# The last 16 rows of Y and Z: made once for all batches, two batches to a group of 32 partitions

## The chip, the core and the metric

The kernel runs on one core of a Trainium2 chip. A core has a matrix engine (TensorE, PE in the profile, its weight loads PEld), a vector engine (VectorE, DVE), a scalar engine (ScalarE, ACT), a general engine (GpSimd, POOL) and an engine for synchronization (SyncE, SP). Transfers are issued by SP, ACT or POOL and carried by 16 DMA engines. The metric is the device time of one execution in microseconds (us). Before the change it is 435.41 us, the median of three runs (435.04, 435.41 and 435.62 us).

## The reference, cut to what matters

```python
# attention: q, k, v are (8 batches, 8 heads, 576 positions, 64), float32
scores = q @ k^T / 8, kept where 0 <= row - column < 64
x = softmax(scores) @ v, laid out as (8, 576, 512)
# spectral mix: w_r, w_i are (64 modes, 512, 512); w_ch is (512, 512)
X = rfft(x, axis=1)[:, :64]
Yr = Xr @ w_r - Xi @ w_i        # per mode
Yi = Xr @ w_i + Xi @ w_r
y = irfft(Yr + 1j * Yi, n=576, axis=1)
u = x + y
out = u + max(u @ w_ch, 0)      # (8, 576, 512), float32
```

The weights are 134 MB, the attention's inputs 28 MB, and the output is 9.44 MB. As u @ w_ch = x @ w_ch + irfft(Y) @ w_ch, the kernel forms Z = Y @ w_ch on the 128 spectral rows (64 modes, real and imaginary part) and adds its inverse transform to x @ w_ch.

## The kernel before, in words

Attention comes first, unit by unit, with the weights of the modes streaming in beside it. The weights are cast to bf16 on the way by transfers that POOL issues, 1 MB at the receiving side each, into two rings of buffers (ringA, ringB) and into lent tiles; L152 to L165 issue the next one when a buffer has been spent. Each group of four modes is multiplied at L188 (`mode_half`), and `finish_group` (L630) turns its 8 spectral rows (4 modes, two parts) for all 8 batches into place. Rows of the spectrum are partitions: `Yall` and `Zall` hold 128 rows by 8 batches by 512 columns, Y in bf16 and Z in 32 bit.

Groups 12 and 13 (`LAST` and `LAST + 1`) are multiplied last. They own rows 96 to 111 of the spectrum, called `rows`, the last 16 rows of the title. Everything else of Y and Z is complete before the last weights land: `batch_job` (L682) makes `Yall` and `Zall` of a batch with these 16 rows at zero, `early_jobs` (L730) already add the inverse transform of those 112 rows to the tiles of batches 0 to 3, in `UE` (for u) and `XW` (for x @ w_ch). The 36 tiles of the output have 128 rows by 512 columns. 16 of them, four for each of batches 0 to 3, are the early tiles; the other 20 are full tiles.

After the last weights the code from L994 runs. For the early tiles the 16 late rows are held apart: batch by batch on their own partitions, YL (bf16, groups of 32 partitions of which 16 are used, batches 0 to 3 at 64, 96, 0, 32, see `YG`) and ZL (at 0, 32, 64, 96, see `ZG`). `trigL` and `trigLr` hold the matching 16 rows of the inverse transform's table once in each of the four groups; eight transfers that SP issues at L951 and L952 put them there, in the middle of the weight stream. `pick` is a 0/1 matrix that moves the rows of the four batches to their groups, `sel` one that compacts the rows of all batches. For the full tiles the late rows have to be in `Yall` and `Zall`: a second product by `sel` (`put_y`, L651) gives them for all batches, ACT casts it into `yst` (L1010), one SP transfer of 128 KB brings them into `Yall` (L1011); a second product with w_ch (L1015, from `trl`) gives the rows of Z, ACT casts them into `zst` (L1020), and one SP transfer of 256 KB brings them into `Zall` (L1021).

`seq` is the order of the tile pairs: four early pairs, then full and early pairs in turn, then full pairs. An early pair (`early`, L903) needs two products with K = 16 for u (L796) and two for z (L803), an addition on DVE (L829), a relu on ACT (L834) and an addition on POOL (L835). A full pair (`full_u`, `full_z`) adds the table's product with `Yall` (L849, L854) and with `Zall` (L868). `plan` puts the output transfers in an order by estimated times. Most are issued by SP at L821, some of the full tiles by ACT. SP takes its instructions in the order of the program, so an issue that waits for its tile holds all that come later.

Of the kernel before, what the change touches and what calls it, by code (L numbers as in the profile page):

```python
# [9 lines left out]
FP32 = mybir.dt.float32  # L10
# [16 lines left out]
def kernel(  # L27
# [10 lines left out]
    nc = tc.nc  # L38
# [32 lines left out]
    pick = consts.tile([128, 32 * NLB + 8], BF16, name="pick")  # L71
# [125 lines left out]
    with tc.manual_schedule():  # L197
# [223 lines left out]
        def trig_steps():  # L421
            yield lambda: ve.memset(trigF[64:128, NTC - 1, :], 0.0)
            yield lambda: ve.memset(trigF[0:64, NTC, :], 0.0)

            yield lambda: ve.tensor_copy(out=sel, in_=ident.rearrange("p (g x) -> p g x", x=32)[:, :, 0:16])
            yield lambda: ve.memset(pick, 0.0)
            yield lambda: zero_xq(1, ve)
            for to in range(0, NLB, 2):
                b = (to + 2) % NLB
                yield lambda to=to, b=b: ve.tensor_copy(  # L430
                    out=pick[:, 8:].rearrange("p (b x) -> p b x", b=NLB)[:, to:to + 2, 0:8].rearrange("p b (g r) -> p b g r", g=4),
                    in_=sel.rearrange("p g (r b) -> p b g r", b=B)[:, b:b + 2])

        trig = list(trig_steps())
        pp = pool("pp", bufs=2, reuse_waits="tile")
# [90 lines left out]
        trigL = zpool.tile([128, 4 * 128], BF16, name="trigL")  # L526
        trigLr = zpool.tile([128, 4 * 128], FP32R, name="trigLr")
        trl = zpool.tile([128, NDCH, 128], FP32R, name="trl")
        trz = zpool.tile([128, NDCH, NLB, 32], FP32R, name="trz")
# [3 lines left out]
        rowpool = pool("rowpool", reuse_waits="tile")  # L533
# [55 lines left out]
        YT = Yall.rearrange("p b (c k) -> p b c k", c=NDCH)  # L589

        rows = slice(8 * LAST, 8 * LAST + 16)
        YG, ZG = (64, 96, 0, 32), (0, 32, 64, 96)

        def yrows(b):
            return Yall[:, b, :]
# [34 lines left out]
        def finish_group(grp, psm):  # L630
            stg = stgpool.tile([128, DM], BF16, name="stg")
            if grp == LAST + 1:
                cast_halves(stg, psm)
            elif grp < EARLY:
                nc.vector.tensor_tensor(out=stg, in0=psm, in1=Yacc[grp], op=ALU.add)  # L635
            else:
                nc.vector.tensor_copy(out=stg, in_=psm)
            i = grp % 2
            end = grp - i == LAST
            if i == 0:  # L640
                late["pt"] = bank("p", [128, NDCH, 128])
                late["py"] = bank("y") if end else None
            pt, py = late["pt"], late["py"]
            lanes = sel.rearrange("p g x -> p (g x)")
# [6 lines left out]
            def put_y():  # L651
                nc.tensor.matmul(out=py[64 * i:64 * i + 64, :], lhsT=lanes, rhs=stg, start=True, stop=True,
                                 tile_position=(0, 64 * i))

            def put_first():
                nc.tensor.matmul(out=late["first"], lhsT=pick[:, 8 - 8 * i:136 - 8 * i], rhs=stg,
                                 start=(i == 0), stop=(i == 1))

            def take():
                nc.scalar.copy(out=trl[:, :, 64 * i:64 * i + 64], in_=pt[:, :, 64 * i:64 * i + 64])  # L660

            def take_first():
                nc.scalar.copy(out=trz[:, :, :, 8 * i:8 * i + 8],
                               in_=pt[:, :, 64 * i:64 * i + 64].rearrange("p c (r b) -> p c b r", b=B)[:, :, 0:NLB])

            def prepare():
                turn()
                if end:
                    put_y()
                    take_first()  # L670
                    take()
                elif i:
                    k0 = 8 * (grp - 1)
                    nc.scalar.copy(out=YT[:, :, :, k0:k0 + 16], in_=pt.rearrange("p c (k b) -> p b c k", b=B))

            if end:
                late[i] = turn, put_first, take, put_y, take_first
            if not (end and i):
                ready.append(prepare)

# [79 lines left out]
                 [XQ[hb].rearrange("p s b m -> p (s b m)").bitcast(FP32).rearrange("p (t e) -> p t e", e=DM)]  # L760
                 for i in range(4)]
        UE_OF = {tile_of(b, c) for b in range(NLB) for c in range(4)}
        AA = [(18 * k // 2 + c, 18 * k // 2 + 4 + c) for k in range(NLB // 2) for c in range(4)]
        BB = [(8, 17), (26, 35)] + [(i, i + 1) for k in range(NLB // 2, B // 2) for i in range(9 * k, 9 * k + 8, 2)]
        assert sorted(i for p in AA + BB for i in p) == list(range(NT))
        X4 = [BB.pop(0) for _ in range(2)]
# [25 lines left out]
        def late_u(n):  # L792
            for i in seq[n]:
                (at, b), = tiles[i][1]
                r = slice(YG[b], YG[b] + 16)
                nc.tensor.matmul(out=pu[i], lhsT=trigL[r, at:at + 128], rhs=YL[r], start=True, stop=True,  # L796
                                 tile_position=(YG[b], 0))

        def late_z(n):
            for i in seq[n]:  # L800
                (at, b), = tiles[i][1]
                r = slice(ZG[b], ZG[b] + 16)
                nc.tensor.matmul(out=ps[i], lhsT=trigLr[r, at:at + 128], rhs=ZL[r], start=False, stop=True,  # L803
                                 skip_group_check=True, tile_position=(ZG[b], 0))

        by_act = {(i, 1) for p in X4 for i in p} | {(p[1], 0) for p in BB[:-1]}
        behind = []
# [128 lines left out]
        for i, (grp, hb) in enumerate(steps[EARLY:]):  # L936
            f, l = grp < EARLY or hb == 0, hb == 1
            if i == EARLY:
                while tables:
                    tables.pop(0)()  # L940
                while jobs or pend:
                    advance()
                close(stmp2, yp, ringB)
                Zall = pool("zall", side="right").tile([2 * NM, B, DM], FP32R, name="Zall")
                x_jobs(pool("xp1", side="right", reuse_waits="tile"), NX0, NT)
                utpool = pool("utpool", side="right", reuse_waits="tile")
                nc.vector.memset(YT[:, :, :, rows], 0.0)
                nc.vector.tensor_scalar(out=trz.rearrange("p c g k -> p c (g k)"), scalar1=0.0, scalar2=None, op0=ALU.mult,
                                        in0=ident.unsqueeze(1).to_broadcast([128, NDCH, 128]))
                for g in range(4):  # L950
                    nc.sync.dma_start(out=trigL[32 * g:32 * g + 16], in_=trigI[rows, 0:512])  # L951
                    nc.sync.dma_start(out=trigLr.bitcast(FP32)[32 * g:32 * g + 16], in_=trigIr.bitcast(FP32)[rows, 0:512])  # L952
                given = 0
            if f:
                psm = [bank("m"), bank("m")] if grp == LAST + 1 else bank("m")
# [35 lines left out]

        turn, put_first, take, put_y, take_first = late[1]  # L994
        tr, first = trl, late["first"]
        turn()
        take_first()
        put_first()
        put_y()
# [11 lines left out]
        nc.sync.dma_start(out=Yall[rows], in_=yst)  # L1011
# [9 lines left out]
        nc.sync.dma_start(out=Zall.bitcast(FP32)[rows], in_=zst.bitcast(FP32))  # L1021
# [43 lines left out]
```

## Time and profile before

| | us |
|---|---|
| median of three runs | 435.41 |
| the profiled execution's own time | 435.39 |
| its span, first to last instruction | 433.6 |
| last weights consumed by PE from | 396.66 |
| first output issued by SP at | 403.17 |
| last product of PE | about 427 |

| engine | busy us | share of the span |
|---|---|---|
| PE | 327.2 | 75% |
| DVE | 229.8 | 53% |
| ACT | 180.1 | 42% |
| POOL | 101.2 | 23% |

The queue q0 carries what POOL issues (the weights and the inputs of the attention, 81.73 MB at the receiving side), q1 what SP issues, q10 what ACT issues. In a timeline a row gives the start and the length in us, the engine, the line, the operation with out<-in, and how many instructions were merged. A q behind an engine's name means its sequencer, which issues transfers. In a row of windows come the busy time of each engine with the number of instructions, the granted TensorE clock, the busy share of the 16 DMA engines (it can go over 1, since packets of one engine overlap) and GB/s.

### The profile page before, as it was taken

To read this page: it belongs to the slowest core of one execution; us is meant where nothing else is said; L and a number is where in the kernel's file an instruction comes from. 1 tells how busy PE (TensorE), PEld (TensorE's weight loads), DVE (VectorE), ACT (ScalarE), POOL (GpSimd) and SP (SyncE) were. 2 spreads that over 40 slices of the span, in tenths; PEclk is the share of its full clock that TensorE was granted. 3 is DMA by queue.
4 is the path that set the end of the run, shared out by engine and by line. 5 is a ranking of instruction groups with operands and counts; after the bars stand their busy time and mean duration, and the time that the engine had idled before them with its cause. 6 is when DMAs were issued, how large, how long until landed. Compare 5 with 4: busy or idle time off the path is not lost.

```text
span 433.6 us, 11034 instructions
## 1 busy us (share of the span) xinstructions
PE 327.2 (75%) x4802; PEld 214.6 (49%) x4802; DVE 229.8 (53%) x472; ACT 180.1 (42%) x322; POOL 101.2 (23%) x150
## 2 busy tenths in 40 slices
PE   6999999998999999963208343767584668779993
PEld 3666667576667666641104121444353345445652
DVE  8588787876776776863104111122131325752994
ACT  5665757565666666520201100122121213434842
POOL 8322222222131231122102100012111112110990
PEclk8899999999999999996557768588889989999998
DMA  8999999999999999999999999999999999993798
GB/s 203 212 211 212 211 211 213 210 211 212 212 213 211 212 212 211 212 213 211 212 259 212 218 212 212 212 210 212 212 209 212 211 212 212 212 212 77 245 365 288
DMA packets 47280, 93.64 MB, mean 216 GB/s; under 512 B 2688, under 2 KB 3136, under 8 KB 47232
## 3 DMA queue, kind: packets, MB, share of 16 engines
q0 software_dynamic: 41008, 81.73, 99.7%
q1 hardware_dynamic: 5328, 9.77, 6.6%
q10 hardware_dynamic: 896, 1.44, 0.9%
q8 instruction: 37, 0.61, 0.5%
q14 instruction: 11, 0.09, 0.1%
HBM read 163.58 MB, written 9.44 MB: 399 GB/s over the span
## 4 chain that ended last, share of the span: by engine, by line
DMA 51%; PE 36%; issue 5%; ACT 3%; DVE 3%; POOL 1%; DVEq 0%; POOLq 0%
DMA wi<-in_moe_w_i_dram 29%; DMA wr<-in_moe_w_r_dram 22%; PE tr L231 6%; PE s L278 4%; PE s L270 3%; PE s L290 3%; PE pt L298 3%; PE psm L188 3%; PE vb L243 3%; PE o L318 2%; PE psz L786 1%; PE pst L786 1%; PE pst L868 1%; PE psz L610 1%; PE px L341 1%
## 5 line engine op out<-in xcount | busy, mean ns | idle before, releaser
L610 PE MATMUL psz<-wch,tr 128*128 128x512 f32 x176 | 62.3, 486 | 11.7 <-DMA wch<-in_moe_w_ch_dram 11.0
L756 DVE CAST xw<-psz 128x512 fp32r<-128x512 f32 x36 | 24.9, 692 | 86.1 <-PE psz L610 86.1
L584 ACT CAST tr<-ptx 128x512 fp32r<-128x512 bf16 x36 | 21.1, 586 | 104.1 <-PE ptx L603 104.1
L282 DVE TENSOR_REDUCE mx<-s 128x4 fp32r<-128x512 f32 x72 | 49.6, 688 | 27.0 <-PE s L278 26.7
L188 PEld LDWEIGHTS <-XQ 128*32 128x32 bf16 x448 | 18.8, 175 | 79.2 <-issue 55.9
L188 PE MATMUL psm<-wi,XQ 128*32 128x512 bf16 x208 | 20.1, 461 | 37.6 <-DMA wi<-in_moe_w_i_dram 37.6
L165 POOL DMA_DIRECT2D wi<-in_moe_w_i_dram x32 | 23.4, 732 | 102.8 <-PE psm L188 74.7
L610 PEld LDWEIGHTS psz<-wch,tr 128*128 128x128 f32 x176 | 36.8, 232 | 18.8 <-issue 11.5
L292 ACT ACTIVATE p<-s 128x512 bf16<-128x512 f32 x72 | 39.7, 603 | 12.9 <-PE s L290 12.9
L165 POOL DMA_DIRECT2D wr<-in_moe_w_r_dram x27 | 20.2, 749 | 97.0 <-PE psm L188 49.0
L188 PE MATMUL psm<-wr,XQ 128*32 128x512 bf16 x184 | 17.9, 465 | 28.3 <-DMA wr<-in_moe_w_r_dram 27.4
L235 ACT COPY kT<-tr 128x576 bf16<-128x576 bf16 x32 | 23.2, 724 | 21.1 <-PE tr L231 21.1
L278 PE MATMUL s<-kT,qT 64*64 64x128 bf16 (+1 forms) x576 | 29.2, 221 | 0.0
L270 PE MATMUL s<-mask_t,ident_bf 128*128 128x512 bf16 x72 | 28.4, 395 | 0.9 <-ACT p L292 0.8
L301 DVE COPY pts<-pt 128x1024 bf16<-128x1024 bf16 (+1 forms) x40 | 25.2, 629 | 5.0 <-PE pt L298 3.6
L235 ACT COPY qT<-tr 128x576 bf16<-128x576 bf16 x32 | 23.3, 728 | 10.6 <-PE tr L231 10.6
L278 PEld LDWEIGHTS <-qT 64*64 64x64 bf16 x576 | 17.8, 107 | 18.0 <-issue 17.5
L635 DVE TENSOR_TENSOR stg<-psm,Yfour 128x512 bf16<-128x512 f32 x10 | 6.9, 690 | 36.8 <-PE psm L188 36.8
L290 PE MATMUL s<-mx,ident_r 128*128 128x512 f32 x72 | 26.2, 437 | 0.0
L235 ACT COPY vT<-tr 128x576 bf16<-128x576 bf16 x32 | 23.3, 727 | 4.3 <-PE tr L231 4.2
L298 PE MATMUL pt<-ident_bf,p 128*128 128x128 bf16 x288 | 23.3, 220 | 1.7 <-issue 1.6
L218 POOL DMA_DIRECT2D rawk<-in_k_dram x15 | 8.1, 539 | 65.3 <-PE tr L231 59.1
(217 smaller groups left out, 607.4 us busy)
## 6 DMA issues: line engine op xcount, KB each, us to landing
wi<-in_moe_w_i_dram POOLq DMA_DIRECT2D x29, 1024.0 KB, 18.6
wr<-in_moe_w_r_dram POOLq DMA_DIRECT2D x27, 1024.0 KB, 17.9
out_dram<-ut SPq DMA_DIRECT2D x23, 256.0 KB, 2.8
rawv<-in_v_dram POOLq DMA_DIRECT2D x16, 288.0 KB, 15.0
rawk<-in_k_dram POOLq DMA_DIRECT2D x15, 288.0 KB, 14.1
rawq<-in_q_dram POOLq DMA_DIRECT2D x15, 288.0 KB, 14.0
x_sb<-in_moe_w_r_dram POOLq DMA_DIRECT2D x2, 1024.0 KB, 15.9
out_dram<-utx SPq DMA_DIRECT2D x5, 256.0 KB, 3.1
```

Source lines behind the costliest of these rows:

```text
L165: nc.gpsimd.dma_start(out=w[:, to:to + len(ps)], in_=src[ps[0]:ps[-1] + 1, HALF * hb:HALF * hb + HALF, :].rearrange("g (p j) e -> p g j e" ...
L188: nc.tensor.matmul(out=ps[32 * g:32 * g + 32, 0:e], lhsT=of.rearrange("k s b m -> k (s b) m")[:, (3 * j + 1 - ri) * B:(3 * j + 5 - ri) * B ...
L231: nc.tensor.transpose(out=pt[ro, j, :], in_=raw[ro, TH * half + j, :], identity=ident_bf[ro, ro])
L235: nc.scalar.copy(out=to, in_=pt.rearrange("p j n -> p n j"))
L270: nc.tensor.matmul(out=s, lhsT=ident_bf, rhs=mask_t[:, mk], start=True, stop=True)
L278: nc.tensor.matmul(out=s[ro, t, lo:128], lhsT=lq, rhs=kT[ro, 64 * n - 64 + lo:64 * n + 64], start=False, stop=True, skip_group_check=True)
L282: nc.vector.tensor_reduce(out=mx, in_=s, axis=AX.X, op=ALU.max, negate=True)
L290: nc.tensor.matmul(out=s, lhsT=ident_r, rhs=mx.unsqueeze(2).to_broadcast([128, 4, 128]), start=False, stop=True, skip_group_check=True)
L292: nc.scalar.activation(out=p[:, 4 * c2:4 * c2 + 4, :], in_=s, func=ACT_F.Exp, scale=EX_SCALE)
L298: nc.tensor.transpose(out=pt[:, t, :], in_=st[u]["p"][:, t, :], identity=ident_bf)
L301: nc.vector.tensor_copy(out=ps[:, 0:nt, :], in_=pt[:, 0:nt, :])
L610: nc.tensor.matmul(out=pz, lhsT=tr[:, c, :], rhs=wch[:, c, :], start=(c == 0), stop=(c == NDCH - 1))
```

## The change

The 16 late rows of Y and Z are made once, for all eight batches, in the layout that the early tiles use, and the same tiles then feed the transfers into `Yall` and `Zall`.

- A group of 32 partitions now holds 16 rows of two batches, rows outer, batches inner. Batches 0 and 1 share a group, 2 and 3, 4 and 5, 6 and 7. `pick` has six blocks of 16 columns instead of four of 8, made by six small DVE copies instead of two.
- The early products have K = 32 instead of 16. Each batch needs the table's rows interleaved with zeros, so `trigL` and `trigLr` have a second plane (one for the even batch, one for the odd), are zeroed by DVE, and are filled by 16 SP transfers instead of 8.
- An early pair is now the same tile of batches b and b + 2 instead of b and b + 1, so that its two products still lie in different groups.
- `put_y`, `take_first`, `trl`, `yst`, `zst` and the second product with w_ch (L1015) are gone. `take` writes all of `trz`.
- The two products of the first pair with YL (`late_u(0)`) stand between the two halves of the product with w_ch.
- Eight SP transfers (per group of two batches one for Y of 32 KB and one for Z of 64 KB) take the place of two. Those of batches 4 to 7 are issued ahead of the first pair's outputs, those of batches 0 to 3 behind them.

```diff
-            for to in range(0, NLB, 2):
-                b = (to + 2) % NLB
-                yield lambda to=to, b=b: ve.tensor_copy(
-                    out=pick[:, 8:].rearrange("p (b x) -> p b x", b=NLB)[:, to:to + 2, 0:8].rearrange("p b (g r) -> p b g r", g=4),
-                    in_=sel.rearrange("p g (r b) -> p b g r", b=B)[:, b:b + 2])
+            to = pick[:, 16:].rearrange("p (n x) -> p n x", x=32)[:, :, 0:16]
+            for n in range(6):
+                yield lambda n=n: ve.tensor_copy(
+                    out=to[:, n].rearrange("p (g r b) -> p g r b", g=4, b=2),
+                    in_=sel.rearrange("p g (r n b) -> p n g r b", n=4, b=2)[:, n % 4])
...
-        AA = [(18 * k // 2 + c, 18 * k // 2 + 4 + c) for k in range(NLB // 2) for c in range(4)]
+        AA = [(tile_of(b, c), tile_of(b + 2, c)) for b in range(NLB // 2) for c in range(4)]
...
-                nc.vector.tensor_scalar(out=trz.rearrange("p c g k -> p c (g k)"), scalar1=0.0, scalar2=None, op0=ALU.mult,
-                                        in0=ident.unsqueeze(1).to_broadcast([128, NDCH, 128]))
+                nc.vector.memset(trigL, 0.0)
+                nc.vector.memset(trigLr.bitcast(FP32), 0.0)
                 for g in range(4):
-                    nc.sync.dma_start(out=trigL[32 * g:32 * g + 16], in_=trigI[rows, 0:512])
-                    nc.sync.dma_start(out=trigLr.bitcast(FP32)[32 * g:32 * g + 16], in_=trigIr.bitcast(FP32)[rows, 0:512])
+                    for x in range(2):
+                        to = slice(32 * g + x, 32 * g + 32, 2)
+                        nc.sync.dma_start(out=trigL[to, x], in_=trigI[rows, 0:512])
+                        nc.sync.dma_start(out=trigLr.bitcast(FP32)[to, x], in_=trigIr.bitcast(FP32)[rows, 0:512])
...
         turn()
-        take_first()
         put_first()
-        put_y()
...
-        zl = [bank("z"), bank("m")]
+        zl = [bank("y"), bank("z")]
+        banks_u(0)
         for h, ps_ in enumerate(zl):
             for c in range(NDCH):
                 nc.tensor.matmul(out=ps_[:, 0:HALF], lhsT=trz[:, c].rearrange("p g k -> p (g k)"),
                                  rhs=wch[:, c, HALF * h:HALF * h + HALF], start=(c == 0), stop=(c == NDCH - 1))
-        yst = rowpool.tile([128, DM], BF16, name="yst")
-        nc.scalar.copy(out=yst, in_=late["py"])
-        nc.sync.dma_start(out=Yall[rows], in_=yst)
+            if h == 0:
+                late_u(0)
         cast_halves(ZL, zl)
-        pz = bank("p")
-        for c in range(NDCH):
-            nc.tensor.matmul(out=pz, lhsT=tr[:, c, :], rhs=wch[:, c, :], start=(c == 0), stop=(c == NDCH - 1))
-        banks_u(0)
-        late_u(0)
         late_z(0)
-        zst = trpool.tile([128, NDCH, 128], FP32R, name="tr").rearrange("p c k -> p (c k)")
-        nc.scalar.copy(out=zst, in_=pz)
-        nc.sync.dma_start(out=Zall.bitcast(FP32)[rows], in_=zst.bitcast(FP32))
+
+        def last_rows(gs):
+            for g in gs:
+                nc.sync.dma_start(out=Yall[rows, 2 * g:2 * g + 2], in_=YL[group_y(2 * g):group_y(2 * g) + 32])
+            for g in gs:
+                nc.sync.dma_start(out=Zall.bitcast(FP32)[rows, 2 * g:2 * g + 2],
+                                  in_=ZL.bitcast(FP32)[32 * g:32 * g + 32])
+
+        last_rows((2, 3))
         take_u(0)
         take_z(0)
+        last_rows((0, 1))
```

More of the change, by code (lines that the diff above doesn't have):

```diff
@@ L70 @@
     sel = consts.tile([128, 4, 16], BF16, name="sel")
-    pick = consts.tile([128, 32 * NLB + 8], BF16, name="pick")
+    pick = consts.tile([128, 16 + 32 * 6], BF16, name="pick")
     trigF = consts.tile([128, NTF, 2 * NM], BF16, name="trigF")
@@ L525 @@
         stgpool = pool("stgpool", bufs=2, reuse_waits="tile")
[L526 to L529, printed above, removed]
+        trigL = zpool.tile([128, 2, 4 * 128], BF16, name="trigL")
+        trigLr = zpool.tile([128, 2, 4 * 128], FP32R, name="trigLr")
+        trz = zpool.tile([128, NDCH, 4, 32], FP32R, name="trz")
         for hb in range(2):
@@ L532 @@
             nc.vector.tensor_copy(out=XL[hb], in_=XQ[hb][:, :, :, 4 * LAST:4 * LAST + 8])
-        rowpool = pool("rowpool", reuse_waits="tile")
         trpool = pool("trpool", bufs=2, reuse_waits="tile")
@@ L591, with group_y, group_z @@
         rows = slice(8 * LAST, 8 * LAST + 16)
-        YG, ZG = (64, 96, 0, 32), (0, 32, 64, 96)
+        lateT = pick[:, 16:144].rearrange("p (n x) -> p n x", x=32)[:, :, 0:16]
+        def group_y(b):
+            return 32 * ((b // 2 + 2) % 4)
+        def group_z(b):
+            return 32 * (b // 2)
         def yrows(b):
@@ L641, in finish_group @@
                 late["pt"] = bank("p", [128, NDCH, 128])
-                late["py"] = bank("y") if end else None
-            pt, py = late["pt"], late["py"]
-            lanes = sel.rearrange("p g x -> p (g x)")
+            pt = late["pt"]
+            lanes = lateT if end else sel
             def turn():
@@ L649, in turn @@
                                      start=True, stop=True)
-            def put_y():
-                nc.tensor.matmul(out=py[64 * i:64 * i + 64, :], lhsT=lanes, rhs=stg, start=True, stop=True,
-                                 tile_position=(0, 64 * i))
             def put_first():
-                nc.tensor.matmul(out=late["first"], lhsT=pick[:, 8 - 8 * i:136 - 8 * i], rhs=stg,
+                nc.tensor.matmul(out=late["first"], lhsT=pick[:, 80 - 16 * i:208 - 16 * i], rhs=stg,
                                  start=(i == 0), stop=(i == 1))
             def take():
[L660 to L664, printed above, removed]
+                nc.scalar.copy(out=trz[:, :, :, 16 * i:16 * i + 16],
+                               in_=pt[:, :, 64 * i:64 * i + 64].rearrange("p c (g x) -> p c g x", x=16))
             def prepare():
@@ L676, in finish_group @@
             if end:
-                late[i] = turn, put_first, take, put_y, take_first
+                late[i] = turn, put_first, take
             if not (end and i):
@@ L794, in late_u @@
                 (at, b), = tiles[i][1]
-                r = slice(YG[b], YG[b] + 16)
-                nc.tensor.matmul(out=pu[i], lhsT=trigL[r, at:at + 128], rhs=YL[r], start=True, stop=True,
-                                 tile_position=(YG[b], 0))
+                r = slice(group_y(b), group_y(b) + 32)
+                nc.tensor.matmul(out=pu[i], lhsT=trigL[r, b % 2, at:at + 128], rhs=YL[r], start=True, stop=True,
+                                 tile_position=(group_y(b), 0))
         def late_z(n):
@@ L801, in late_z @@
                 (at, b), = tiles[i][1]
-                r = slice(ZG[b], ZG[b] + 16)
-                nc.tensor.matmul(out=ps[i], lhsT=trigLr[r, at:at + 128], rhs=ZL[r], start=False, stop=True,
-                                 skip_group_check=True, tile_position=(ZG[b], 0))
+                r = slice(group_z(b), group_z(b) + 32)
+                nc.tensor.matmul(out=ps[i], lhsT=trigLr[r, b % 2, at:at + 128], rhs=ZL[r], start=False, stop=True,
+                                 skip_group_check=True, tile_position=(group_z(b), 0))
         by_act = {(i, 1) for p in X4 for i in p} | {(p[1], 0) for p in BB[:-1]}
@@ L990 @@
                     given += 1
-        turn, put_first, take, put_y, take_first = late[1]
-        tr, first = trl, late["first"]
+        turn, put_first, take = late[1]
+        first = late["first"]
         turn()
-        take_first()
         put_first()
-        put_y()
         ZL = trpool.tile([128, NDCH, 128], FP32R, name="tr").rearrange("p c k -> p (c k)")
```

## The prediction

> **What bounds the kernel now.** The slices of the page come first, then the chain of waits, then the DMA queues around the places that the change touches.
>
> ```profile
> DMA  8999999999999999999999999999999999993798
> GB/s 203 212 211 212 211 211 213 210 211 212 212 213 211 212 212 211 212 213 211 212 259 212 218 212 212 212 210 212 212 209 212 211 212 212 212 212 77 245 365 288
> DMA 51%; PE 36%; issue 5%; ACT 3%; DVE 3%; POOL 1%; DVEq 0%; POOLq 0%
> ```
>
> From about 12 us to 391 us the DMA engines are full at one rate, 212 GB/s, and the chain that ended last rests on weight transfers. So up to the landing of the last weights (396.6 us) the kernel is a stream: compute added there is free while it keeps its place behind the stream, and every transfer added there delays it.
>
> Two answers on the DMA queues show that price. The first window (233 to 245 us) holds the table transfers of L951 and L952, the second is the next 12 us without them; the row of the tile `trigL` shows what SP pays to issue one.
>
> ```profile
> q0 software_dynamic: 1207, 2.40, 106.1%
> q1 hardware_dynamic: 256, 0.20, 6.6%
> ...
> q0 software_dynamic: 1281, 2.54, 112.1%
> ```
>
> ```profile
> L951 SPq DMA_DIRECT2D trigL<-trigI x4: 588/610/1054, 230.0 to 238.4; - x4
> ```
>
> While q1 moved 0.20 MB, the weights' queue moved 2.40 MB in place of 2.54. The reader is to see that the little transfers are paid by the stream.
>
> Last the end, in windows and in SP's timeline:
>
> ```profile
> 396.70:402.00 5.30, 4.89 (x32) 2.93 (x31) 2.60 (x5) 3.19 (x8) 0.15 (x1) 1.00 0.09 25
> 402.00:405.00 3.00, 3.00 (x22) 1.61 (x19) 3.00 (x6) 2.94 (x7) 3.00 (x3) 1.00 0.74 156
> 405.00:408.00 3.00, 3.00 (x20) 1.89 (x17) 2.67 (x6) 2.21 (x5) 3.00 (x3) 1.00 0.62 228
> 408.00:420.00 12.00, 12.00 (x65) 7.28 (x63) 10.73 (x19) 7.12 (x14) 12.00 (x11) 1.00 1.03 382
> 426.00:430.00 4.00, 1.05 (x5) 0.53 (x3) 1.76 (x4) 0.81 (x2) 0.00 (x0) 1.00 1.04 391
> ```
>
> ```profile
> 399.15 0.63 SPq L1011 DMA_DIRECT2D Yall<-yst  x1
> 401.30 0.58 SPq L1021 DMA_DIRECT2D Zall<-tr  x1
> 403.17 1.58 SPq L821 DMA_DIRECT2D out_dram<-utx  x2
> 405.65 5.77 SPq L821 DMA_DIRECT2D out_dram<-ut  x9
> ```
>
> PE is always busy up to 427 us, but from 408 us on the DMA engines are full as well, with the output, and remain so for three microseconds after PE's last product. So the end is where the output's bytes run out: 36 tiles of 0.262 MB at 382 GB/s, 0.69 us a tile. What counts there is how many tiles are through before the engines fill up, not how fast PE is later. POOL too has no gap from 402 to 420 us: it adds the 16 early tiles at 1.29 us each, so the order on SP is paced by it at first.
>
> **The change, part by part.** The sum is against the profiled execution, 435.39 us, which lies 0.02 below the median.
>
> *Eight more table transfers in the stream.* 0.20 MB more on q1. The eight of before cost the stream 2.54 - 2.40 = 0.14 MB, and 0.14 / 212 GB/s = 0.66 us. From 245 to 391 us the engines' share is 1.12 without a break, so nothing gives this back, and the last weights land 0.66 us later. Bounds: 0.40 (the slowest engine is hit less than the mean) to 0.95 us (all of q1's bytes at the stream's rate). I take 0.66, measured for the same transfers.
>
> *DVE's two memsets and four more copies into `pick`, one table of zeros less.* About 1 us of DVE, beside the stream: at 240 us DVE waits for products of PE (gaps of 0.7 to 2.6 us before the casts of L756), and in the attention the transfers land 14 to 18 us after their issue, so a DVE delay far below that starves no queue. Nothing; without that cover 1 us at most.
>
> *Late rows, PE and ACT.* Gone from PE are L652 (0.33 us on the chain of waits) and L1015 (0.93), from ACT L663 (0.27), L1010 (0.58) and L1020 (0.59). But little of it was what the first relu waited for. Before: the turned rows are read by L663 (397.99 to 398.26), the halves L1007 run from 398.44 to 399.66, ACT casts the second half by 400.12, L803 starts at 400.53, the relu L834 at 401.17. After: the copy that the halves wait for is the larger one (L660's 0.38 in place of 0.27, +0.11), the two products of `late_u(0)` stand between the halves (+0.22, half of the 0.43 that four such full-width products take on the chain), and ACT casts by 400.46. L803 then starts at 400.55, as before, and the relu starts when its product is out, about 401.05: 0.12 us earlier, since L1020 no longer stands ahead of it. So POOL's row of additions starts 0.12 us earlier and all behind it too. Bounds: 0 to 0.5 us gained. That K is 32 costs nothing: a product's time follows its 512 columns (0.38 us with K = 16 at L796 and with K = 128 at L849), and the pair (b, b + 2) keeps two different groups, in which the two products overlap as before.
>
> *Six more issues on SP, and their place.* SP's issue of a transfer from SBUF to SBUF takes 0.63 (L1011), 0.58 (L1021) and 0.61 (L951), whether it has 16 partitions or 128. The four for batches 4 to 7 fit between YL (ready 398.9), ZL (400.5) and the first output; they end near 401.7, and `Zall`, which L868 needs at 405.6, lands no later than now. The four for batches 0 to 3 are behind the second output on SP: that is issued at 404.29 (404.41 less 0.12) and ends at 404.63, then 4 x 0.63 = 2.5 us, so the third output, issued at 405.65 now, waits on SP until 407.15. Those queued behind it follow at the 0.43 us that consecutive issues take (406.90, 407.33 and on), and SP is level again at the eighth, 409.4. The engines idle meanwhile: now the third output's data are through before they fill up at about 408, then not. That is one tile of 0.69 us more to move after 408, and a start some 0.3 us later: 1.0 us. Against it I set the share below 1 between 420 and 426 us (0.98 there against 1.03), which a longer queue fills: 0.25. Taken: +0.75. Bounds: 0.0 (these issues are as quick as the outputs', 0.33 to 0.43 us) and 1.4 (two tiles displaced).
>
> The rows for batches 0 to 3 are first needed by tile (8, 17) at 416 us; landing by 410 they delay nobody. The wait of SP for YL and ZL stands ahead of the first output alone, which is later anyway.
>
> [...]
>
> **Sum:** 435.39 + 0.66 (stream) + 0.75 (output's queue, with the 0.12 of the earlier start in it) = 436.8 us.
>
> **Rivals.**
> *SP's queue hides it.* The four issues cost 0.4 us each, or the lag is made up before 426 us. For it: outputs take 0.33 to 0.43. Against: all ten issues from SBUF to SBUF took 0.53 us or more. Then the third output goes at 406.2 and the gain of 0.1 stands: 435.39 + 0.66 - 0.1 = 436.0, no change that can be told.
> *PE's saving reaches the end (faster).* The place is 397.7 to 401 us, the price 0.33 + 0.93 = 1.26 us off. It decides if the products, not the output's transfers, set the end, and the table transfers are covered: 435.39 - 1.26 = 434.1. For it: PE has no gap up to 427 us. Against: shares of 1.03 and 1.04 in the last windows, and the last issues land 4 us after issue where the early ones took 2.5. With the stream's price it is 434.8, no change that can be told.
> *The lag feeds back.* A buffer of `ut` is used again after seven pairs, and DVE already waited 0.28 us for an output's landing at 417.37; a lag of 1 us at that place stops ACT or DVE, and SP's order passes it on: 1.0 more, 437.8.
> [...]
>
> **How the numbers follow.** No change means within 0.2%, which is about what a measurement of this kernel can tell, 434.5 to 436.3 us. The forecast has 0.62 (its own range 436.1 to 437.6, with 0.04 of it below 436.3); the hidden queue 0.2; PE's saving 0.07 (0.04 of it as faster); the feedback 0.1; transfers in series 0.01. Slower: 0.58 + 0.1 + 0.01 = 0.69; same: 0.04 + 0.2 + 0.03 = 0.27; faster 0.04. The range from 435.4 to 437.9 takes in the hidden queue with the stream's lower bound (0.40) and most of the feedback, and leaves out PE's saving and the series.
>
> **What would show it.** Sixteen table transfers near 240 us and q0 lower by twice the amount of now; the last weights consumed from about 397.3. From there: the first relu 4.4 us later (4.51 now), four issues in a row of about 0.6 each between the second and the third output, a dip of the DMA share just then, and 1.03 after it to the end. I am wrong if the weights land at 396.6 again, if those issues take 0.4, or if the DMA share falls below 1 in the last 10 us, so that products set the end.

## The result, and the profile after

The changed kernel takes 437.86 us (median of four runs, 437.71 to 438.12) and the kernel before 435.27 on the same chip: the ratio is 1.0056 (95% interval 1.0039 to 1.0072), and the medians differ by 2.6 us. The profiled execution took 437.90 us with a span of 436.1, against 435.39 and 433.6 before. The forecast was 436.8 with a range up to 437.9, and "slower" at 0.69: the sign and both places were right, one of the two terms was too small, and the time lies only 0.04 us inside the range.

The page after, its slices and its chain:

```profile
DMA  8999999999999999999999999999999999992698
GB/s 206 211 211 211 211 213 210 212 211 212 212 211 211 213 211 212 211 212 212 212 259 211 212 211 213 211 223 213 213 210 210 211 213 211 212 206 54 219 368 299
DMA 52%; PE 32%; issue 7%; ACT 3%; DVE 3%; POOL 1%; ACTq 0%; SPq 0%; DVEq 0%; POOLq 0%
```

The stream still runs at 212 GB/s up to its end. What differs is behind it: the dip in the 37th slice is deeper (54 GB/s, 77 before), and the 38th is lower (219, 245 before). The table transfers were foretold near 240 us; they are found by their tile at 281 to 291 us, behind the two new memsets on DVE (the row of the first):

```profile
L947 SPq DMA_DIRECT2D trigL<-trigI x8: 587/588/615, 281.1 to 290.3; - x8
L942 DVE MEMSET trigL<- x1: 485/485/485, 280.6 to 280.6; 128x512 uint32 x1
```

The DMA queues from 281 to 295 us (14 us, with all sixteen transfers) and from 295 to 307 us (12 us, without any):

```profile
q0 software_dynamic: 1366, 2.72, 102.8%
q1 hardware_dynamic: 489, 0.38, 10.7%
...
q0 software_dynamic: 1278, 2.53, 111.8%
```

At 2.53 MB per 12 us the first window would have carried 2.95 MB; it carried 2.72. Sixteen transfers took 0.23 MB from the stream, where 0.28 was foretold.

PE's timeline at the end of the stream (start, length, engine and line, out<-in, idle before):

```profile
397.17 0.60 PE L188 MATMUL psm<-wi,XL 128*32 128x256 bf16 x4 [0.62 <-DMA wi<-in_moe_w_i_dram]
```

The last weights are consumed from 397.17 us, 396.66 before: 0.51 later. Below, times in the tail are counted from this row and called "after the weights", so that stream and tail can be told apart. The first relu comes 4.53 after the weights (4.51 before), and the last output has landed 37.74 after the weights (35.87 before). So of the 2.51 us between the two profiled executions 0.51 came before the last weights and 1.87 behind them; the remaining 0.13 lies around these rows, nearly all of it behind the last landing.

SP's timeline behind the weights, and the one issue that began at 405.96 by itself:

```profile
401.14 1.20 SPq L1013 DMA_DIRECT2D Zall<-tr  x2
403.69 1.59 SPq L815 DMA_DIRECT2D out_dram<-utx  x2
405.33 2.22 SPq L1011 DMA_DIRECT2D Yall<-stg  x2
407.60 1.23 SPq L1013 DMA_DIRECT2D Zall<-tr  x2
408.92 3.29 SPq L815 DMA_DIRECT2D out_dram<-ut  x6
```

```profile
405.96 1.59 SPq L1011 DMA_DIRECT2D Yall<-stg  x1
```

The four issues stand between the second and the third output, as foretold. Three took 0.58 to 0.59 us, but the second took 1.59, and the third output was issued at 408.92, 11.75 after the weights (8.99 before, 10.49 foretold). Windows of the same stretch, in the columns of those of before:

```profile
405.00:407.00 2.00, 2.00 (x12) 1.52 (x10) 1.63 (x4) 2.00 (x4) 2.00 (x2) 1.00 0.56 191
407.00:410.00 3.00, 3.00 (x17) 1.83 (x16) 2.67 (x5) 2.10 (x5) 3.00 (x4) 1.00 0.27 66
410.00:423.00 13.00, 11.88 (x63) 7.08 (x63) 9.79 (x17) 6.00 (x11) 12.29 (x10) 1.00 1.03 381
423.00:428.00 5.00, 4.95 (x28) 3.18 (x28) 4.90 (x9) 2.64 (x5) 1.17 (x1) 1.00 0.97 316
428.00:434.00 6.00, 1.36 (x7) 0.80 (x5) 2.28 (x5) 1.17 (x3) 0.00 (x0) 0.82 1.04 382
```

From 407 to 410 us the DMA engines moved 66 GB/s; the kernel before had been at 382 from 408 on. From 410 us they are as full as they were. In the 13.34 us behind the last weights (up to 410.0 us before) the queues carried 2.05 MB before and 1.14 MB after, by the trace's sums. The missing 0.91 MB at 382 GB/s are 2.4 us; the tail became 1.87 longer. (The row transfers carry as many bytes before and after, 384 KB, so what is missing is output.)

### The profile page after: what moved, and what is told of

Read it like the earlier page. It is cut to its first block, busy times and chain, and to the rows that moved or that the text cites. A ratio compares the mean times of both kernels' runs of the same rounds, so it can differ in the third digit from the quotient of the medians.

```text
span 436.1 us, 10992 instructions
## 1 busy us (share of the span) xinstructions
PE 324.2 (74%) x4751; PEld 215.2 (49%) x4796; DVE 231.7 (53%) x477; ACT 178.9 (41%) x318; POOL 101.1 (23%) x150
## 4 chain that ended last, share of the span: by engine, by line
DMA 52%; PE 32%; issue 7%; ACT 3%; DVE 3%; POOL 1%; ACTq 0%; SPq 0%; DVEq 0%; POOLq 0%
DMA wr<-in_moe_w_r_dram 33%; DMA wi<-in_moe_w_i_dram 18%; PE tr L231 5%; PE s L278 4%; PE s L290 3%; PE pt L298 3%; PE vb L243 3%; PE psm L188 3%; PE o L318 2%; PE s L270 2%; PE px L341 1%; ACT qT L235 1%; PE pst L780 1%; ACT p L292 1%; DMA out_dram<-ut 1%
## 5 line engine op out<-in xcount | busy, mean ns | idle before, releaser
L614 PE MATMUL psz<-wch,tr 128*128 128x512 f32 x176 | 61.3, 480 | 11.7 <-DMA wch<-in_moe_w_ch_dram 11.0
L188 PE MATMUL psm<-wi,XQ 128*32 128x512 bf16 x208 | 21.1, 481 | 36.2 <-DMA wi<-in_moe_w_i_dram 36.2
L188 PE MATMUL psm<-wr,XQ 128*32 128x512 bf16 x184 | 19.2, 497 | 25.6 <-DMA wr<-in_moe_w_r_dram 24.8
L330 DVE TENSOR_TENSOR x_sb<-o,r 128x512 bf16<-128x512 f32 x32 | 22.1, 691 | 1.1
```

Source lines behind the costliest of these rows:

```text
L188: nc.tensor.matmul(out=ps[32 * g:32 * g + 32, 0:e], lhsT=of.rearrange("k s b m -> k (s b) m")[:, (3 * j + 1 - ri) * B:(3 * j + 5 - ri) * B ...
L330: nc.vector.tensor_tensor(out=xo.rearrange("p c (h d) -> p c h d", d=64), in0=ov[:, :, :, 0:64], in1=rb, op=ALU.mult)
```

## The experiments

Every kernel is compared with the kernel before on the same chip. "MB" is what all queues moved in the 13.34 us behind the last weights; the middle columns are of the profiled execution, counted from the last weights. The row of before has the time of the first set of runs; in the three later ones it took 435.20, 435.17 and 435.18.

| kernel | third output issued | MB | last output landed | last weights at | time, median | ratio (95%) |
|---|---|---|---|---|---|---|
| before | 8.99 | 2.05 | 35.87 | 396.66 | 435.27 | |
| after | 11.75 | 1.14 | 37.74 | 397.17 | 437.86 | 1.0056 (1.0039 to 1.0072) |
| after_again | 11.16 | 1.37 | 37.04 | 397.44 | 438.32 | 1.0072 (1.0056 to 1.0088) |
| e1_tables | 8.99 | 2.05 | 35.78 | 397.45 | 435.95 | 1.0018 (1.0010 to 1.0027) |
| e2_rows | 11.59 | 1.40 | 37.92 | 397.35 | 437.75 | 1.0056 (1.0044 to 1.0068) |
| e3_spread | 9.00 | 1.93 | 35.77 | 397.58 | 436.38 | 1.0032 (1.0017 to 1.0046) |
| e4_pe_spread | 10.50 | 1.62 | 36.89 | 396.15 | 435.47 | 1.0004 (0.9995 to 1.0012) |
| e6_fetch | 10.74 | 1.52 | 37.09 | 397.29 | 438.13 | 1.0068 (1.0053 to 1.0082) |

The theory: the loss is the sum of two parts that do not depend on each other, the table transfers in the stream and the four issues on SP between the outputs. Its rivals: the products, or the outputs' landing fed back through the buffers, set the end. The column of the last weights is of one execution each and scatters by some tenths of a us whatever was changed (e2_rows below); the medians measure the whole time, not its parts.

**One part alone: the tables.** The kernel before, with eight more table transfers into the 16 partitions of each group that it does not use.

```diff
+                for g in range(4):
+                    nc.sync.dma_start(out=trigL[32 * g + 16:32 * g + 32], in_=trigI[rows, 0:512])
+                    nc.sync.dma_start(out=trigLr.bitcast(FP32)[32 * g + 16:32 * g + 32], in_=trigIr.bitcast(FP32)[rows, 0:512])
```

> The kernel before with the change's eight additional table transfers alone: the same 16 rows are also copied into the 16 unused partitions of each group, which no product reads. Nothing else differs. Theory (the stream of weights pays for them): the last weights are consumed 0.4 to 0.8 us later and the kernel takes 0.6 us more, 435.9 where the kernel before takes 435.3. Rival (the stream has room for them and the whole loss is made after the last weights): 435.3, the last weights consumed at 396.7 as before.

435.95 against 435.20: 0.78 us by the ratio (0.44 to 1.17), and the tail is as before (35.78). The stream's term of 0.66 stands. The trace shows it at its place too, if one asks when the weights' queue q0 has moved a given number of MB, and compares with the kernel before: e1_tables is 0.1 us behind at 48 MB, ahead of the table transfers, and 0.7 behind at 52 MB. The sixteen transfers of the changed kernel cost 1.14 us between 58 and 62 MB (1.13 to 1.15 in after_again, e3_spread and e6_fetch); the eight of the kernel before, which the changed kernel does not have there, 0.61 between 48 and 50 MB.

**One part alone: the rows.** The kernel before, with four transfers behind the second output, of the sizes of the change, into places that nobody reads.

```diff
         take_u(0)
         take_z(0)
+        for g, t in enumerate((trl.rearrange("p c k -> p (c k)"), trz.rearrange("p c g k -> p (c g k)"))):
+            nc.sync.dma_start(out=t.bitcast(BF16)[rows].rearrange("p (b e) -> p b e", b=2), in_=yst[32 * g:32 * g + 32])
+        for g in range(2):
+            nc.sync.dma_start(out=wch.bitcast(FP32)[rows, 2 * g:2 * g + 2], in_=zst.bitcast(FP32)[32 * g:32 * g + 32])
```

> The kernel before with four additional SP transfers behind the second output, of the sizes of the change (two of 32 KB, two of 64 KB, each from 32 partitions to rows 96 to 111), into tiles that nobody reads any more. The products, the tables and the two large row transfers are those of before. Theory (SP's queue holds the third output, and the output's transfers lose their start): the third output is issued 2.5 to 3.5 us after the second one's issue ends, the DMA engines are full some 1.5 us later, and the kernel takes 1.4 to 2.0 us more, 436.7 to 437.3. First rival (as in the prediction, SP is held for 4 x 0.63 us and no more): 0.75 more, 436.1. Second rival (the loss comes from the products and copies of the change, not from SP): 435.3.

437.75 is above what was expected (436.7 to 437.3). It is as slow as the whole change, 1.0056, although all products of the kernel before are in it. SP's timeline of this kernel:

```profile
405.54 0.60 SPq L1025 DMA_DIRECT2D trl<-yst  x1
406.19 1.36 SPq L1025 DMA_DIRECT2D trz<-yst  x1
407.65 1.19 SPq L1027 DMA_DIRECT2D wch<-tr  x2
408.94 3.31 SPq L821 DMA_DIRECT2D out_dram<-ut  x6
```

The third output comes late again, at 11.59, and again one of the four issues is long. So four such transfers at this place make a tail's loss of this size without any of the change's products. They also add 0.20 MB to what the queues carry: of output 0.65 + 0.20 = 0.85 MB are missing, 2.2 us at 382 GB/s, where the tail is 2.05 longer. Whether it is their place or their bytes, the next kernel tells. The two parts alone come to 0.78 + 2.44 = 3.2 us by the ratios, where the whole change measured 2.4 in one set of runs and 3.1 in another (after_again). The stream of e2_rows came 0.69 late in the profile, although nothing was added to it: the last weights of one profiled execution scatter by as much as the term looked for, and the end of the stream in one profile cannot measure that one.

**The issues moved out of the way.** The changed kernel with six of its eight row transfers ahead of the first output and the last two one by one behind the first and the second.

```diff
-        last_rows((2, 3))
...
+        for g in (2, 3, 0, 1):
+            y_row(g)
+        for g in (2, 3):
+            z_row(g)
         take_u(0)
-        take_z(0)
-        last_rows((0, 1))
+        take_z(0, z_row)
```

> The changed kernel with the same transfers issued elsewhere: the four of Y and two of Z (batches 4 to 7) ahead of the first output, one of Z between the first and the second output, one of Z behind the second, so that no more than one stands ahead of the third. Theory: the loss on SP goes, that of the table transfers stays: 0.4 to 0.8 us over the kernel before, 435.7 to 436.1, with the third output about 8.9 to 9.2 us after the last weights are consumed (11.75 in the changed kernel, 8.99 before). Rival (the products and copies or the additional bytes are to blame): 437.5 to 437.9 as the changed kernel.

```profile
404.62 0.57 SPq L1015 DMA_DIRECT2D Zall<-tr  x1
405.35 0.48 SPq L815 DMA_DIRECT2D out_dram<-utx  x1
405.87 0.56 SPq L1015 DMA_DIRECT2D Zall<-tr  x1
406.58 5.41 SPq L815 DMA_DIRECT2D out_dram<-ut  x8
```

Six of the transfers now stand ahead of the first output, and the last two one by one between outputs that had to wait for POOL anyway (SP waited 0.8 us for it ahead of the second and again ahead of the third output in the kernel before). The third output goes 9.00 after the weights and the last lands at 35.77: the whole loss of the tail is gone, with all the bytes and products of the changed kernel still there, so that it was the place of the issues that cost it. 1.0032 is left, 1.4 us, in an execution whose last weights came 0.92 late. The tables' price from above explains 0.78 of that; the other 0.6 was not traced further (the interval begins at 1.0017, 0.7 us). The median, 436.38, lies above the 435.7 to 436.1 that was expected.

**The tables without the transfers.** As the kernel above, and both planes of the tables made by one PE product each with a 0/1 matrix, copied out by DVE and ACT; no table transfer is left, the eight of before included.

```diff
...
+                for x in range(2):
+                    pb = bank("y")
+                    nc.tensor.matmul(out=pb, lhsT=trz[:, x].rearrange("p g k -> p (g k)"), rhs=trigIr[:, 0:512],
+                                     start=True, stop=True)
+                    nc.vector.tensor_copy(out=trigL[:, x], in_=pb)
+                    nc.scalar.copy(out=trigLr[:, x], in_=pb)
```

> As e3_spread, and in addition the two planes of the table are made by two products on PE with a 0/1 matrix (rows to places), each copied by DVE (bf16) and ACT, about 280 us: all sixteen table transfers are gone, also the eight that the kernel before has. Theory (table transfers cost the stream 0.08 us each): 1.1 to 1.3 us less than e3_spread and 0.5 to 0.7 us less than the kernel before, 434.6 to 434.8, last weights consumed near 396.0. Rival (the stream has room): as e3_spread.

435.47, no change from before, and not the 434.6 to 434.8 that was expected. The weights were early (396.15), but the last of the row transfers, which stood just ahead of the third output, took 2.07 us to issue, and the tail lost 1.0:

```profile
403.95 0.49 SPq L815 DMA_DIRECT2D out_dram<-utx  x1
404.48 2.07 SPq L1019 DMA_DIRECT2D Zall<-tr  x1
406.65 5.37 SPq L815 DMA_DIRECT2D out_dram<-ut  x9
```

**What holds an issue for 1.0 to 2.1 us?** In each of these executions a transfer of 16 KB on q8, the queue of instructions, stood near the long issue. The page of the changed kernel has 37 of them:

```profile
q8 instruction: 37, 0.61, 0.5%
```

Between two of them lie 251 instructions of PE on average, weight loads counted (166 to 319). One of them began at 405.82 in the changed kernel and took 1.40 us, at 406.10 in e2_rows (1.07), at 404.67 in e4_pe_spread (1.50) and at 405.35 in the kernel before (1.09), whose third output was issued at 405.65 in 0.33 us. The kernel before has a held issue too, 0.28 us behind the beginning of a q8 transfer at 235.09 us (0.96), among the table transfers; it is the longest of the row of L951 that the prediction shows:

```profile
235.37 1.05 SPq L951 DMA_DIRECT2D trigL<-trigI  x1
```

e1_tables and e2_rows have one at the same place (1.22 and 1.23). To move the transfer at 405.82, 40 tiny products were put on PE near 280 us in the changed kernel, with the changed kernel itself beside it.

```diff
+                pad = bank("y")
+                for _ in range(40):
+                    nc.tensor.matmul(out=pad[:, 0:16], lhsT=ident_bf, rhs=ident_bf[:, 0:16], start=True, stop=True)
```

> The changed kernel once more, beside the next ones on the same chip: 2.2 to 2.7 us over the kernel before, 437.4 to 437.9.

> The changed kernel with 40 tiny products (16 columns each, result read by nobody) added on PE near 280 us, in the weights' shadow. They move PE's later instructions by 80 places, so that the 16 KB fetch of instructions that stood at 405.8 us in the changed kernel should come about 8 us earlier, near 398 us, where no transfer is under way. Theory (a DMA engine held by this fetch stopped the second of the four row issues on SP, 1.59 us in place of 0.6): all four issues take 0.55 to 0.65, the third output is issued 10.7 us after the last weights are consumed (11.75 in the changed kernel), and the kernel takes 0.8 to 1.1 us less than the changed kernel, 436.6 to 437.0; what then stays over the kernel before after the last weights, 0.8 to 1.0 us, is the price of four plain issues. Rival (the long issue comes from the row transfers themselves): an issue of 1.2 us or more stays among the four, and the time is that of the changed kernel.

The changed kernel again has a long issue (1.01), and its third output is at 11.16; its median of 438.32 is above the 437.4 to 437.9 expected. With the products put in, SP's timeline is even:

```profile
405.45 1.22 SPq L1014 DMA_DIRECT2D Yall<-stg  x2
406.71 1.22 SPq L1016 DMA_DIRECT2D Zall<-tr  x2
408.03 3.98 SPq L815 DMA_DIRECT2D out_dram<-ut  x7
```

The transfer of instructions now comes at 398.37, all four issues take 0.58 or 0.59, and the third output is at 10.74, as expected. So the long issue goes with that transfer; that it holds a DMA engine, as the theory has it, no run shows. But the time did not follow: 438.13 against 438.32, not the 436.6 to 437.0 expected, and the intervals overlap almost wholly; nor did the tail, 37.09 against 37.04. Another transfer of instructions now comes at 423.63, among the outputs, beside an issue of 1.26 us. What the long issue is worth in the time is therefore not shown; the four issues of ordinary length alone cost the tail 37.09 - 35.87 = 1.22 us. The profiled execution of e6_fetch is the fastest of its five (437.46), as that of after_again is of its six (437.50); what the others lose beyond it was not traced.

**Towards a faster kernel.** Four more kernels sought the 0.5 to 0.7 us that the table transfers should return. e7_best is e4_pe_spread with 34 tiny products; e9_late_pe makes its two products 6 and 8 half groups later and sends the last row of Z behind the third output; e8_before_pe and e10_before_late_pe are the kernel before with its eight table transfers replaced by one product, at once or 6 half groups later.

```diff
-                    nc.sync.dma_start(out=trigL[32 * g:32 * g + 16], in_=trigI[rows, 0:512])
-                    nc.sync.dma_start(out=trigLr.bitcast(FP32)[32 * g:32 * g + 16], in_=trigIr.bitcast(FP32)[rows, 0:512])
...
+                if half == n0 + 6:
+                    pb = bank("y")
+                    nc.tensor.matmul(out=pb, lhsT=trl[:, 0], rhs=trigIr[:, 0:512], start=True, stop=True)
+                    nc.vector.tensor_copy(out=trigL, in_=pb)
+                    nc.scalar.copy(out=trigLr, in_=pb)
```

> As e4_pe_spread (no table transfers, the rows' issues spread), with 34 tiny products on PE as in e6_fetch to move the fetch of instructions. Theory: the issue of 2.07 us goes, the third output comes 9.0 us after the last weights are consumed, the stretch from there to the last landing is 35.8 us as in the kernel before, and the saving of the table transfers is left: 0.5 to 0.8 us under the kernel before, 434.4 to 434.7. Rival (the long issue is the row transfers' own): as e4_pe_spread, 0.2 over the kernel before.

> The kernel before with its table rows put into the four groups by one product on PE with a 0/1 matrix and two copies, so that its eight table transfers are gone and nothing else. Theory: the stream gets their 0.4 to 0.8 us back, 434.4 to 434.8. Rival (the stream has room for them): as before, 435.2.

> As e4_pe_spread, but the two products that make the table's planes come six and eight half groups later (about 310 and 320 us), when the tables that they read are long done, so that PE does not wait in front of them; and the last Z transfer is issued behind the third output. Theory (in e4, e7 and e8 the stream won the table transfers' time by 243 us and lost it again where PE waited for its new work): the stream keeps 0.5 to 0.6 us over the kernel before, the stretch behind the last weights is 35.8 us as before, 434.5 to 434.8. Rival (the stream's end does not follow from the table transfers): 435.2 or more.

> As e8_before_pe, with the product that makes the table six half groups later. Theory (the eight transfers' price was won and lost again in e8): 0.4 to 0.7 us under the kernel before, 434.5 to 434.8, with the weights' queue 0.5 us ahead of the kernel before from 50 MB on to the end. Rival (the eight transfers of before cost nothing, only more than eight do): 435.2.

| kernel | third output issued | last output landed | last weights at | time, median (lowest to highest) | ratio (95%) |
|---|---|---|---|---|---|
| e7_best | 9.01 | 36.28 | 396.54 | 437.85 (435.80 to 441.44) | 1.0069 (1.0043 to 1.0094) |
| e8_before_pe | 9.00 | 35.44 | 396.81 | 435.40 (435.11 to 435.68) | 1.0001 (0.9992 to 1.0010) |
| e9_late_pe | 9.00 | 35.92 | 396.24 | 435.37 (434.69 to 440.65) | 1.0041 (1.0008 to 1.0074) |
| e10_before_late_pe | 8.98 | 35.20 | 396.21 | 435.14 (434.65 to 436.64) | 1.0002 (0.9993 to 1.0010) |

All four missed. By the MB that q0 has moved, each of them gains about 0.6 us between 48 and 50 MB, where the eight transfers are gone. e8_before_pe has lost it again at 62 MB, and e7_best 1.65 us between 58 and 60 MB, where PE makes the table; e9_late_pe and e10_before_late_pe, which make it later, keep it to 81 MB. In e10_before_late_pe the profiled execution took 434.71 with its last weights 0.45 early, as expected, but the median of twelve is that of the kernel before. So adding eight table transfers costs a measurable 0.78 us in the median, and taking eight away returns nearly as much in the stream of a profile, but nothing that can be measured in the median; why the medians do not follow stays open. The twelve times of e9_late_pe fall into two sets, seven from 434.69 to 435.39 and five from 437.78 to 440.65, and those of e7_best are scattered; their cause was not found. No kernel beat the one before by more than the measurement can tell.

## Why the prediction was right or wrong

The direction and the two places were foreseen. That the time lies inside the range is luck: its upper end was set by the rival that the lag feeds back, the theory's own range ended at 437.6, and its two terms at their upper bounds, 0.95 and 1.4, give 437.74, below the 437.86 measured. The changed kernel measured again, 438.32, lies outside.

*The stream's term, 0.66 us: right.* 0.78 us (0.44 to 1.17) by e1_tables; at its place in the trace 1.14 for sixteen transfers against 0.61 for eight, so 0.53; 0.51 by the last weights of the profiled execution, which scatter as much. The place in time was wrong (281 us, not 240, since DVE comes to the first memset only at 280.6), without effect, as the stream is equally full there (in the changed kernel a share of 1.12 at 212 GB/s from 226 to 280 us and 1.12 at 211 from 296 to 391). The lower bound of 0.40 was an assumption on the slowest DMA engine that no run shows; the interval by e1_tables begins at 0.44.

*DVE's memsets at nothing: nothing speaks against it.* They took 0.49 and 0.91 us beside the stream, and e1_tables, which has none of them, pays no less in the stream than the change does. No kernel has the memsets alone.

*An earlier relu by 0.12 us: wrong, and small.* It came 4.53 after the weights, 0.14 later than foretold. PE's timeline of the changed kernel shows why:

```profile
398.93 0.73 PE L1002 MATMUL psy<-wch,trz 128*128 128x256 f32 x4 [0.46 <-ACT trz L659]
399.60 0.39 PE L790 MATMUL psm<-stg,trigL 32*128 32x512 bf16 x2
399.92 0.73 PE L1002 MATMUL psz<-wch,trz 128*128 128x256 f32 x4
```

The first half starts 1.76 us after the weights, 0.13 earlier than the sum had it. But from its start to the end of the second half it is 1.72 us, where the same halves took 1.22 before: the two products of `late_u(0)` between them cost 0.50 and not 0.22. The second cast on ACT is late by as much (400.74, 3.57 after the weights in place of 3.43), and with it the z products and the relu. What was removed from ACT had not been the limit.

*Four issues of 0.63 between the second and the third output: right in place and mechanism, too small in price.* This is the step that failed. The sum had the third output wait until 407.15, 10.49 after the weights, at a price of 0.75 us with a bound of 1.4; the tail became 1.87 us longer. Two terms in it were off.

First the lateness. Without the long issue it is 10.74 (e6_fetch): 0.14 us of the earlier relu that did not come, and the rest from gaps between the issues. With the long issue it is 11.16 to 11.75. The prediction took 0.61 for L951 from a row that goes up to 1.05, and did not ask what made that one issue long. It stood beside a q8 transfer, and another such transfer stood at 405.35 us in the same trace, where the four issues were to go.

Second the price of the lateness. The prediction counted one tile and 0.3 us, took 0.25 off again for a share that a longer queue would fill, and so charged 0.75 for 1.5 us. What was measured, with the missing MB of the table at 382 GB/s beside it: e6_fetch 1.22 for 1.75 us late (0.53 MB, 1.4 us), after_again 1.17 for 2.17 (0.68 MB, 1.8 us), the changed kernel 1.87 for 2.76 (0.91 MB, 2.4 us), e2_rows 2.05 for 2.60 (0.85 MB of output, 2.2 us). It is 0.5 to 0.8 us for each us of lateness where the sum took 0.5, and the missing bytes overstate it by up to a half. The 0.25 did not last: the changed kernel makes good a part where the kernel before has its dip (0.69 MB are missing 28 us behind the weights), and loses it in a dip of its own (0.85 MB at 30 us). The window from 423 to 428 us has a share of 0.97 at only 316 GB/s there, so a longer queue did not raise what the engines moved.

*The rival that the lag feeds back* (437.8 us) came nearest in time, and its sign is in the trace. In the chain of the changed kernel:

```profile
413.69 3.03 DMA out_dram<-ut
...
416.81 0.59 ACT ut L856
```

ACT waited 1.34 and 1.47 us for an output's landing before it could write `ut` again, and PE had 1.12 us without work in the 13 us from 410. But the DMA engines were full all that time, at 1.03, and the missing bytes do not grow: 0.91 MB at 410 us, and 0.87 MB over the 32 us behind the weights. Nor do such waits go with the loss. From 408 to 428 us ACT waits 3.5 us for landings in the changed kernel; it waits 5.3 in e3_spread, whose tail is that of before, and 0.7 in after_again, whose tail is 1.17 longer. The feedback happened, and nothing of the loss has to be charged to it.

*PE's saving reaches the end:* it did not. e3_spread leaves out the same products and has the tail of before, 35.77 against 35.87. *SP's queue hides it:* it did not, in after and in e2_rows (third output at 11.75 and 11.59 after the weights, 8.99 before). *Transfers in series* (0.01 of the chances): no run shows small transfers that wait for each other to land. Four cost the tail 1.22 us (e6_fetch), or 2.05 with one of them held (e2_rows), and in the changed kernel two of 64 KB issued at 407.60 and 408.23 landed 2.2 us after their issue. The one transfer of 256 KB into `Zall` that the kernel before has landed 4.2 us after its issue, its outputs of 256 KB issued from 403 to 412 us after a median of 2.7; no run shows why.

## What to carry to other kernels

Where one queue issues everything in program order and the transfers set the end, count each issue at its own row's length and put it where the queue waits for something else: here four small transfers behind the second output cost 1.2 to 1.9 us in the tail, and nothing when they stood ahead of the outputs and in SP's waits for POOL (35.77 us from the weights to the last landing, 35.87 before). Read the longest issue of a row as well as its median. Price the delay by the bytes that are not moved before the engines fill up, as an upper bound, and give no credit for a later dip unless a row shows that more in the queue fills it. The products and casts taken away beside this queue were worth nothing here, and the small transfers added to the full stream cost 0.78 us for 0.20 MB, not far from the 0.95 that these bytes are at 212 GB/s.

## What the runs showed of the hardware that was not expected

An SP issue from SBUF to SBUF that stood beside a 16 KB transfer of instructions (q8) took 1.01, 1.36, 1.59 or 2.07 us in the tail of four kernels (after_again, e2_rows, the changed kernel, e4_pe_spread), and 1.05 among the table transfers of the kernel before, where such issues take 0.51 to 0.69 otherwise; with the transfer moved away all four were 0.58 or 0.59 (e6_fetch). In e3_spread it held an output's issue for 1.20 us, without harm, as the next output was not ready before. Not every issue near one is held: in the kernel before, e1_tables, e8_before_pe and e10_before_late_pe an output was issued in 0.33 or 0.34 us, 0.10 to 0.34 us behind the beginning of one. Nor is every long issue held by one: near the end of every kernel two to four issues of outputs take 1.0 to 1.25 us with no such transfer beside them. As 40 products more moved the transfer from 405.8 to 398.4 us, 0.19 us for each product, a few products more or fewer can, as an estimate from this one pair, put one among the issues, and a change may meet one that it has nothing to do with.
